# A Fourier mixing layer and a tanh-shrink MLP on one core: the beginning put in another order

## The chip, the cores and the metric

The kernel runs on one core of a Trainium2 chip. The core has TensorE (PE, matrix products; PEld is its loading of weights), VectorE (DVE), ScalarE (ACT), GpSimd (POOL) and SyncE (SP), which each run their own list of instructions in order and wait for each other through semaphores. Transfers are issued from SP's, ACT's and GpSimd's queues and carried by 16 DMA engines. The metric is device time in microseconds (us); less is better.

## The reference

A batch of 8 sequences of 3008 tokens by 256 channels is filtered in the frequency domain, and the result goes token by token through an MLP whose activation is h - tanh(h).

```python
def _attn_ref(x, filt_r, filt_i):
    X = np.fft.rfft(x, axis=1)              # x: (8, 3008, 256)
    F = (filt_r + 1j * filt_i)[None, :, :]  # (1505, 256)
    Y = X * F
    return np.fft.irfft(Y, n=x.shape[1], axis=1).astype(np.float32)

def _moe_ref(x, w_in, w_out):               # x: (24064, 256)
    h = x @ w_in                            # (256, 2048)
    g = h - np.tanh(h)
    return (g @ w_out).astype(np.float32)   # (2048, 256)
```

The two weight matrices arrive as 64-bit floating-point numbers, which the kernel reads as integers; x and the filters are 32-bit.

## The kernel before

**The transform.** 3008 = 64 x 47. A transform of one batch is three stages of small matrix products with a trip through DRAM after the first and the second: `first` multiplies 24 slices of x (128 x 256 each) with the matrices f and stores to `ct1`; `middle` takes seven rounds, one for each group of rows ("slot", six of 120 rows and a last of 48), and stores to `ct2`; `last` loads e2 from `ct2`, multiplies with the matrices g and leaves u in SBUF for the MLP.

**A round of the middle stage** has four parts. `forth` (L316 to L332) loads nothing itself; it multiplies a2 with two constant matrices into the bank pa, copies the half of v = 1 with ACT, and lets VectorE form sum and difference (L330, L331). `filtered` (L334 to L350) is the complex product with the filter: two products of 1024 columns (L340, L343), a difference and a sum of 512 (L345, L346, engine `by2`), then another sum and difference on VectorE (L348, L349). `back` (L352 to L365) multiplies with the constant matrices into pe, copies to e1 with ACT and stores from ACT's queue. For batch 0 the seven rounds run in the beginning, by themselves, with `by2` GpSimd; for the batches 1 to 7 they are spread over the dense rounds of the batch before, with `by2` VectorE.

**The weights** come in eight quarters, four of w_in (tile wu) and four of w_out (wd), each of two pieces of 128 x 512 numbers. `converted` turns a piece into 32-bit floating point: a load of 512 KB (raw), three VectorE operations (L145, L146, L148), two operations that VectorE (L152, L154) or ACT (L157, L158) does, then VectorE again (L160, L162, L164 and two or three at L171). After both pieces of a quarter GpSimd forms four sums of weights (`sums`, L201 to L204), because the MLP's products are done with seven block products where eight would be usual. Three generators spread the conversion: `weights_alone` (all on VectorE), `weights` (shared with ACT, several pieces under way) and `weights_slow` (one step at a time, all on VectorE).

**The beginning (L783 to L899), batch 0.** SP issues, in turn, a third of f and a third of x, three times, and the mats; GpSimd's queue the filter of round 0 and four raw pieces. Between the thirds of the first stage `weights_alone` converts quarters 0 and 1. Then seven rounds follow; in each, the products back of the preceding round and the steps of `weights` for quarters 2 to 4 stand between the parts. Quarter 5 follows behind the last round. A filter buffer is one of three (`filt[g % 3]`), filled from GpSimd's queue with six transfers a round.

**The dense rounds.** Each of 48 groups of tokens takes four rounds U (192 in all, and two more to empty the pipeline). In round U TensorE does `up(U)` (seven pairs of products into x, y and z), the other engines do `shrink(U - 1)` (the activation by ACT and VectorE) and TensorE does `down(U - 2)`. VectorE adds the banks into h (L512, L529, L537, L545), ACT copies from the banks (L495). Inside a round five calls of `t(k)` place other work: at most one step of a transform whose place in the plan has come (`planned`, in units of a fifth of a round), one step of `weights_slow`, and one step of a copy of the filters in DRAM. The plan spreads `first` of batch 1 over the places 0.2 to LEAD/2, that of batch 2 over LEAD/2 to LEAD, and `middle` of batch 1 from LEAD to LAG, with LEAD 30 and LAG 104. Quarters 6 and 7 are converted here. wd's quarter n is first used in round n + 2, wu's quarter n in round n.

Of the kernel before, what the change touches and what calls it, by code (L numbers as in the profile page):

```python
# [9 lines left out]
F32 = mybir.dt.float32  # L10
# [11 lines left out]
SG = 5  # L22
# [14 lines left out]
LEAD, LAG = 30, 104  # L37
# [53 lines left out]
def kernel(  # L91
# [119 lines left out]
    def weights(tiles, quarters, ahead):  # L211

        jobs = parts_of(quarters)
        began = []
        for job in jobs[:ahead]:
            began.append(begun(tiles, job))
            yield
        for k in range(len(jobs) + 1):
            if k < len(jobs):
                next(began[k])  # L220
            if k > 2 and k % 2:
                sums(quarters[k // 2 - 1])
            yield
            if k < len(jobs):
                next(began[k])
            if k > 0:
                for _ in began[k - 1]:
                    pass
            if k + ahead < len(jobs):
                began.append(begun(tiles, jobs[k + ahead]))  # L230
            yield
        sums(quarters[-1])
        yield

    def weights_alone(tiles, quarters, queue):

        jobs = parts_of(quarters)
        began = [begun(tiles, job, True, queue) for job in jobs[:2]]
        yield
        for k in range(len(jobs)):  # L240
            if k + 2 < len(jobs):
                began.append(begun(tiles, jobs[k + 2], True, queue))
            for _ in began[k]:
                pass
            if k % 2:
                sums(quarters[k // 2])
            yield

    def weights_slow(tiles, quarters):

        jobs = parts_of(quarters)
        began = [begun(tiles, job, True) for job in jobs[:2]]
        yield
        for k in range(len(jobs)):
            for _ in began[k]:
                yield
            if k + 2 < len(jobs):
                began.append(begun(tiles, jobs[k + 2], True))
            if k % 2:
                sums(quarters[k // 2])  # L260
                yield
# [55 lines left out]
    def forth(g, at, z):  # L317
# [4 lines left out]
        for v in (1, 0):  # L322
# [4 lines left out]
            if v:  # L327
                ACT.copy(xy[:, 2:4], pa)
                yield xy
# [4 lines left out]
    def filtered(g, xy, ft, by, by2):  # L334
# [4 lines left out]
        nn = tr.tile([KM, 4, DM], F32, tag="nn", bufs=1, name="nn")[0:n]  # L339
        by.tensor_mul(nn.rearrange("p (x v) c -> p x v c", v=2), ab,  # L340
                      fv[:, :, 0:1].to_broadcast([n, 2, 2, DM]))
        yield
# [23 lines left out]
    def middle(b, z):  # L366
# [4 lines left out]
        for g in range(len(SLOTS)):  # L371
# [5 lines left out]
            if before:  # L377
                next(before[0])
                yield
            next(there)  # L380
# [405 lines left out]
    with tc.tile_pool(name="tr", bufs=2) as tr, tc.manual_schedule():  # L786
        with tc.tile_pool(name="pro", bufs=1) as pro, \
# [11 lines left out]
            def first0(xt, c):  # L799

                for i in range(2):
                    r = 8 * c + 4 * i
                    a1 = pro.tile([128, 4, DM], F32, tag="a1", bufs=4, name="a1")
# [21 lines left out]

            def tiles0(k, dtype, n):
# [10 lines left out]
            V.memset(exp_b, 0.0)  # L837
            xs = []
            for c in range(3):
                nc.sync.dma_start(f0[:, 8 * c:8 * c + 8], f_d[:, 1024 * c:1024 * c + 1024])  # L840
                xs.append(load_x(big([128, 8, DM], F32, "x0"), 0, 8 * c, 8))

            ACT.activation(exp_b, exp_b, AF.Arctan)
            V.memset(exp_b, -896.0)
            ws = weights_alone(tiles0, range(2), G)

            for t in filt:
                G.memset(t[0:SG, 2:4], 0.0)
            nc.sync.dma_start(mats, mats_d)
            fts = {0: filters_of(0)}  # L850
            next(ws)
            for c in range(3):
                for k, _ in enumerate(first0(xs[c], c)):
                    if k == 3:
                        next(ws)
            fts[1] = filters_of(1)
            turned_rows()
            late_ws = weights(tiles0, range(2, 5), 3)
            a2 = {0: load_a2(0, 0), 1: load_a2(0, 1)}
            for _ in range(2):  # L860
                next(late_ws)
            for _ in ws:
                pass
            ws = late_ws
            next(ws)
            waiting = iter(())
            last_g = len(SLOTS) - 1
            for g in range(last_g + 1):
                if g + 1 < last_g:
                    fts[g + 2] = filters_of(g + 2)  # L870
# [3 lines left out]
                if g + 1 < last_g:  # L874
                    a2[g + 2] = load_a2(0, g + 2)
                done = filtered(g, xy, fts.pop(g), V, G)
                for _ in waiting:
                    next(ws, None)
                for _ in done:
                    pass  # L880
                next(ws, None)
                waiting = back(0, g, xy, z0)
                if g == last_g - 1:
                    fs = first(1, z1)
                    next(fs)
                    ws_gap = weights_alone(tiles0, range(5, 6), nc.sync)
                    next(ws_gap)
            for _ in waiting:
                pass
            e2s[0] = load_e2(*groups[0])  # L890
            for w in (ws, ws_gap):
                for _ in w:
                    pass
# [5 lines left out]
        with tc.tile_pool(name="dn", bufs=2) as dn, \  # L899
# [15 lines left out]
            def tiles1(k, dtype, n):  # L915

                tag, bufs = {"raw": ("ft", 2), "it": ("xy", 2), "pt": ("nn", 1), "st": ("e1", 2),
                             "ft": ("a2", 2)}[k]
                return tr.tile([128, n], dtype, tag=tag, bufs=bufs, name=k)

# [16 lines left out]
            late, copies = weights_slow(tiles1, range(6, 8)), filters_d()  # L937
# [3 lines left out]
            next(late)  # L941
# [123 lines left out]
```

## Time and profile before

| | |
|---|---|
| median of 3 runs | 2806.02 us (2805.11 to 2806.81) |
| the profiled execution | 2806.34 us, of which its span is 2804.6 us |
| TensorE busy | 2693.7 us, 96% of the span |
| VectorE / ACT / GpSimd busy | 1673.3 / 1723.7 / 1388.3 us |
| moved by the DMAs | 215.44 MB, 77 GB/s over the span |

A profile shows one execution. Its rows give busy time by engine, for the whole span or for a stretch of it; groups of instructions by source line with count and mean time; who waited for whom; and a chain of waits, followed back from the last instruction. "L345" is line 345 of the kernel before. A product in 32-bit floating point shows as two records, so four products appear as x8. The granted clock is the share of TensorE's full rate that it was given. A queue's "us to landing" is the median from the issue of a transfer until its data are there.

### The profile page before, as it was taken

The page shows a single profiled execution, that of the slowest core. Times are in us where ns is not written, and L with a number is a line of the kernel's source. Part 1 is how long each engine was busy: PE and PEld are TensorE (multiplying, and loading weights), DVE is VectorE, ACT ScalarE, POOL GpSimd, SP SyncE. Part 2 cuts the span into 40 slices and gives each one's busy share as a digit, 9 for nine tenths or more (in the row PEclk, how much of TensorE's full clock was granted, in tenths as well). Part 3 has the DMA queues.
Part 4 walks back from the last instruction along what each step waited for, and adds up shares of the span by engine and source line. Part 5 has one row for each costly group of instructions (what it writes and reads, how often), then busy time and mean ns, then how long its engine had stood idle before and what let it go on. Part 6 is the DMA issues. An engine that isn't in the chain of part 4 may idle for free.

```text
span 2804.6 us, 36366 instructions
## 1 busy us (share of the span) xinstructions
PE 2693.7 (96%) x12830; PEld 2366.6 (84%) x12830; DVE 1673.3 (60%) x2094; ACT 1723.7 (61%) x2583; POOL 1388.3 (50%) x1195
## 2 busy tenths in 40 slices
PE   4499999999999999999999999999999999999998
PEld 3388888988889888998889888898888988899887
DVE  4755675666556665556656666566654766554545
ACT  2155666666666666666666666666666666666665
POOL 4455545544445444545455444454544554454452
PEclk8699999999999999999999999999999999999999
DMA  9475213323132332234223331242222222111010
GB/s 247 116 245 145 69 43 78 95 69 82 51 95 74 80 91 55 74 74 104 56 62 73 101 87 47 60 116 66 78 53 67 54 64 55 30 24 33 21 26 18
DMA packets 341634, 215.44 MB, mean 77 GB/s; under 512 B 227736, under 2 KB 300988, under 8 KB 341251
## 3 DMA queue, kind: packets, MB, share of 16 engines
q1 hardware_dynamic: 296851, 154.15, 23.1%
q10 hardware_dynamic: 39504, 50.61, 5.8%
q0 software_dynamic: 5088, 8.28, 1.1%
q8 instruction: 103, 1.69, 0.3%
q14 instruction: 88, 0.72, 0.1%
HBM read 137.83 MB, written 78.12 MB: 77 GB/s over the span
## 4 chain that ended last, share of the span: by engine, by line
PE 87%; DVE 6%; DMA 2%; issue 2%; ACT 2%; POOL 1%; ACTq 0%; SPq 0%; DVEq 0%; POOLq 0%
PE o L614 38%; PE x L489 22%; PE z L489 11%; PE y L489 5%; PE pa L325 3%; PE pe L359 3%; PE pu L455 3%; PE pf L293 2%; DMA x<-in_x_dram 1%; DMA ct<-a 1%; DVE xy L349 1%; DVE h L570 1%; DVE h L545 1%; DVE h L512 1%; DVE xy L348 0%
## 5 line engine op out<-in xcount | busy, mean ns | idle before, releaser
L614 PE MATMUL o<-t,wd 128*128 128x256 f32 (+1 forms) x3072 | 775.0, 375 | 0.0
L469 POOL TENSOR_TENSOR t<-h 128x512 f32<-128x512 f32 (+1 forms) x190 | 261.8, 1378 | 893.6 <-DVE h L570 865.6
L570 DVE TENSOR_TENSOR h<-h,y 128x1024 f32<-128x1024 f32 (+1 forms) x384 | 511.2, 1331 | 293.0 <-ACT y L566 292.5
L614 PEld LDWEIGHTS o<-t,wd 128*128 128x128 f32 x3072 | 582.7, 190 | 69.7 <-issue 2.4
L489 PE MATMUL x<-tu,wu 128*128 128x256 f32 (+1 forms) x2304 | 586.0, 377 | 2.1 <-ACT s L495 1.7
L614 PE MATMUL o<-h,wd 128*128 128x256 f32 (+1 forms) x2304 | 583.8, 376 | 3.2 <-DVE h L570 3.2
L489 PEld LDWEIGHTS x<-tu,wu 128*128 128x128 f32 x2304 | 430.1, 190 | 64.5 <-ACT u L495 8.8
L614 PEld LDWEIGHTS o<-h,wd 128*128 128x128 f32 x2304 | 434.1, 190 | 55.5 <-DVE h L570 4.3
L495 ACT COPY s<-x 128x512 f32<-128x512 f32 (+1 forms) x192 | 110.9, 577 | 511.6 <-PE x L489 498.2
L560 ACT ACTIVATE y<-h 128x1024 f32<-128x1024 f32 (+1 forms) x384 | 400.2, 1042 | 12.5 <-ACT a L294 5.1
L563 ACT ACTIVATE y<-y 128x1024 f32<-128x1024 f32 (+1 forms) x384 | 399.5, 1040 | 12.6 <-ACT a L294 0.4
L566 ACT ACTIVATE y<-y 128x1024 f32<-128x1024 f32 (+1 forms) x384 | 400.0, 1042 | 4.7
L529 DVE TENSOR_TENSOR h<-z,u 128x512 f32<-128x512 f32 (+1 forms) x192 | 130.1, 678 | 275.2 <-ACT u L495 274.3
L495 ACT COPY u<-x 128x512 f32<-128x512 f32 (+1 forms) x384 | 219.5, 572 | 94.1 <-PE x L489 70.7
L471 POOL TENSOR_TENSOR t<-h 128x512 f32<-128x512 f32 (+1 forms) x190 | 271.2, 1427 | 0.0
L470 POOL TENSOR_TENSOR t<-h,t 128x512 f32<-128x512 f32 (+1 forms) x190 | 263.6, 1387 | 14.9
L472 POOL TENSOR_TENSOR t<-t,h 128x512 f32<-128x512 f32 (+1 forms) x190 | 268.0, 1411 | 0.0
L537 DVE COPY h<-x 128x512 f32<-128x512 f32 (+1 forms) x192 | 130.4, 679 | 162.3 <-PE x L489 161.8
L489 PE MATMUL x<-ut,wu 128*128 128x256 f32 (+1 forms) x768 | 193.9, 375 | 0.7 <-DVE h L537 0.7
L489 PE MATMUL y<-ut,wu 128*128 128x256 f32 (+1 forms) x768 | 193.8, 375 | 0.0
L489 PE MATMUL z<-ut,wu 128*128 128x256 f32 (+1 forms) x768 | 193.7, 375 | 0.0
L489 PE MATMUL z<-tu,wu 128*128 128x256 f32 (+1 forms) x768 | 193.7, 375 | 0.0
(116 smaller groups left out, 3051.5 us busy)
## 6 DMA issues: line engine op xcount, KB each, us to landing
e<-ct SPq DMA_DIRECT2D x48, 512.0 KB, 4.3
a<-ct SPq DMA_DIRECT2D x48, 480.0 KB, 5.2
ct<-e ACTq DMA_DIRECT2D x96, 240.0 KB, 2.8
ct<-a ACTq DMA_DIRECT2D x84, 256.0 KB, 2.7
x_sb<-in_x_dram SPq DMA_DIRECT2D x161, 128.0 KB, 4.1
ft<-filt SPq DMA_DIRECT2D x42, 480.0 KB, 6.8
out_dram<-ot SPq DMA_DIRECT2D x1248, 16.0 KB, 1.5
gt<-g SPq DMA_DIRECT2D x48, 256.0 KB, 3.2
```

What stands on the lines that cost most here:

```text
L469: by.tensor_sub(t[0], b[0][1], b[0][0])
L470: by.tensor_sub(t[1], b[1][1], t[0])
L471: by.tensor_sub(t[2], b[1][1], b[0][1])
L472: by.tensor_sub(t[3], t[1], b[1][0])
L489: nc.tensor.matmul(bank[:, k], wu[:, q - 1, (2 * u + k) * 128:(2 * u + k + 1) * 128], rhs[q - 1], start=(first and k == 0), stop=True, ski ...
L495: ACT.copy(t, X)
L537: V.tensor_copy(h[:, 2, :, 0:w], X)
L560: ACT.activation(y[k], ht[k], AF.Arctan, scale=TURN)
L563: ACT.activation(y[k], y[k], AF.Tanh, scale=BEND)
L566: ACT.activation(y[k], y[k], AF.Square, scale=SCALE, accum_out=y_sums[:, 2 * U + k // 2:2 * U + k // 2 + 1])
L570: V.tensor_mul(ht[k], ht[k], y[k])
L614: nc.tensor.matmul(product(q), wd[:, q - 1, (2 * u + k) * 128: (2 * u + k + 1) * 128], rhs[q - 1][:, k], start=(u == 0 and k == 0 and q == ...
```

## The change

- The first loads: f and mats are issued from ACT's queue, x from SP's. GpSimd clears its filter buffers first, loads the filter of round 0, and then waits, through a copy of one element (`gate`), until the second third of x has landed; only then it issues raw pieces 0 and 1, the filter of round 1, raw pieces 2 and 3 and the turned rows.
- The pieces of quarters 0 to 2 (six) are converted in the beginning by `convert`, which shares with ACT: four ahead of round 0, behind all products of the first stage, and two behind the last round. `weights` and `weights_alone` are gone.
- Middle stage of batch 0: `by2` is VectorE; the products forth of round g + 1 are issued ahead of the filter of round g; nn has two buffers. In rounds 0 to 5 the last sum and difference are left out, and `back0` reaches the same result with twice the products: each pe half is a product with nn[k] plus a product with nn[2 + k], accumulated in PSUM. The last round keeps them.
- `weights_slow` shares with ACT and takes quarters 4, 3, 5, 6, 7 (ten pieces). It begins in the beginning of the kernel with its first two loads, and has two steps in each `t(k)`.
- The plan: `first` of batch 1 from 6 to 20, of batch 2 from 20 to LEAD, and LEAD is 34.

```diff
-LEAD, LAG = 30, 104
+LEAD, LAG = 34, 104
...
 def weights_slow(tiles, quarters):
         jobs = parts_of(quarters)
-        began = [begun(tiles, job, True) for job in jobs[:2]]
+        began = [begun(tiles, job) for job in jobs[:2]]
...
+            def back0(g, nn):
+                way = ways(g, 1)
+                for v in range(2):
+                    pe = z0("pe", [128, 2, DM])[0:KM]
+                    for k in range(2):
+                        nc.tensor.matmul(pe[:, k], way[2 * v + k], nn[:, k],
+                                         start=True, stop=False)
+                        nc.tensor.matmul(pe[:, k], way[3 - k if v else 0], nn[:, 2 + k],
+                                         start=False, stop=True)
+                    e1 = tr.tile([KM, 2, DM], F32, tag="e1", bufs=2, name="e1")
+                    ACT.copy(e1, pe)
+                    ACT.dma_start(rows(ct2, 0, g, 2 * v, 2), e1)
...
+            for t in filt:
+                G.memset(t[0:SG, 2:4], 0.0)
             xs = []
             for c in range(3):
-                nc.sync.dma_start(f0[:, 8 * c:8 * c + 8], f_d[:, 1024 * c:1024 * c + 1024])
+                ACT.dma_start(f0[:, 8 * c:8 * c + 8], f_d[:, 1024 * c:1024 * c + 1024])
                 xs.append(load_x(big([128, 8, DM], F32, "x0"), 0, 8 * c, 8))
+            ACT.dma_start(mats, mats_d)
...
             fts = {0: filters_of(0)}
+            gate = cst.tile([1, 1], F32, name="gate")
+            G.tensor_copy(gate, xs[1][0:1, 0, 0:1])
+            jobs = parts_of(range(3))
+            began = [begun(tiles0, job, queue=G) for job in jobs[:2]]
+            fts[1] = filters_of(1)
+            began += [begun(tiles0, job, queue=G) for job in jobs[2:4]]
+            turned_rows()
+            def convert(k):
+                for _ in range(1 if k + 1 < len(jobs) else 0):
+                    next(began[k + 1])
+                for _ in began[k]:
+                    pass
+                if k % 2:
+                    sums(k // 2)
+                if k + 4 < len(jobs):
+                    began.append(begun(tiles0, jobs[k + 4], queue=G))
             for c in range(3):
-                for k, _ in enumerate(first0(xs[c], c)):
-                    if k == 3:
-                        next(ws)
+                for _ in first0(xs[c], c):
+                    pass
             a2 = {0: load_a2(0, 0), 1: load_a2(0, 1)}
+            next(began[0])
+            for k in range(4):
+                convert(k)
...
+            there = {0: there0(0)}
             for g in range(last_g + 1):
+                if g + 2 <= last_g:
+                    fts[g + 2] = filters_of(g + 2)
+                    a2[g + 2] = load_a2(0, g + 2)
+                if g < last_g:
+                    there[g + 1] = there0(g + 1)
+                next(there[g][0])
+                xy = there.pop(g)[1]
-                done = filtered(g, xy, fts.pop(g), V, G)
-                for _ in waiting:
-                    next(ws, None)
-                for _ in done:
-                    pass
-                next(ws, None)
-                waiting = back(0, g, xy, z0)
+                done = filtered(g, xy, fts.pop(g), V, V, pro)
+                nn = next(done)
+                for _ in range(2):
+                    next(done)
+                if g < last_g:
+                    back0(g, nn)
+                else:
+                    next(done)
+                    for _ in back(0, g, xy, z0):
+                        pass
                 if g == last_g - 1:
                     fs = first(1, z1)
                     next(fs)
-                    ws_gap = weights_alone(tiles0, range(5, 6), nc.sync)
-                    next(ws_gap)
+                    late = weights_slow(tiles1, (4, 3, 5, 6, 7))
+                    next(late)
             e2s[0] = load_e2(*groups[0])
+            for k in range(4, len(jobs)):
+                convert(k)
...
-                f = [spread(NX, *((0.2, LEAD / 2) if b == 1 else (LEAD / 2, LEAD) if b == 2
+                f = [spread(NX, *((6, 20) if b == 1 else (20, LEAD) if b == 2
                                   else (0.2, LAG)), firsts, b, first)
...
                     next(late, None)
+                    next(late, None)
```

`there0(g)` runs `forth(g)` up to its products and ACT's copy. The buffers of the first stage's result (a1) go from four to three.

87 lines of the change are left out of this document (17 added, 70 removed).

## The prediction

> **What bounds the kernel now.** The page comes first: TensorE's row of the 40 slices, and the chain of waits by engine.
>
> ```profile
> span 2804.6 us, 36366 instructions
> ...
> PE   4499999999999999999999999999999999999998
> ...
> PE 87%; DVE 6%; DMA 2%; issue 2%; ACT 2%; POOL 1%; ACTq 0%; SPq 0%; DVEq 0%; POOLq 0%
> ```
>
> TensorE is full in every slice but the first two, and the diff leaves the later batches as they are. So the work that the change moves can only pay in the beginning, until the first dense product. Next the busy times by stretch there: up to VectorE's first addition of the middle stage (50.67), to that stage's last one, to the first dense product at 143.8, and the first three dense rounds.
>
> ```profile
> 0.00:50.67 50.67, 19.65 (x57) 14.90 (x58) 16.68 (x42) 9.11 (x15) 22.25 (x39) 0.83 0.95 262
> 50.67:132.00 81.33, 37.63 (x98) 26.14 (x98) 60.00 (x93) 17.43 (x30) 44.96 (x54) 0.67 0.55 144
> 132.00:143.80 11.80, 11.62 (x45) 8.24 (x43) 8.39 (x23) 1.69 (x3) 3.17 (x5) 0.68 0.48 154
> 143.80:154.50 10.70, 9.67 (x46) 7.84 (x46) 7.33 (x20) 3.89 (x7) 3.11 (x6) 1.00 0.86 270
> 154.50:166.80 12.30, 9.98 (x47) 7.82 (x45) 7.30 (x17) 7.31 (x13) 4.00 (x6) 1.00 0.88 270
> 166.80:183.50 16.70, 14.76 (x73) 13.44 (x73) 13.46 (x23) 11.27 (x19) 7.12 (x8) 1.00 0.79 236
> ```
>
> After its length a row gives busy time of PE, PEld, DVE, ACT, POOL, then granted clock, DMA share, GB/s. The first 50.67 us belong to the DMAs (share 0.95). The next 81.33 us belong to nobody: the DMAs are half used, TensorE half busy, VectorE 74%. That is a chain. The waits of that stretch and one turn of the chain say which:
>
> ```profile
> PE pe L359 <- DVE xy L348: 43.7, 7, 8.9
> DVE xy L348 <- POOL nn L346: 20.3, 7, 4.5
> ...
> 53.44 1.24 DVE xy L343
> ...
> 54.76 1.25 POOL nn L345
> 56.01 1.22 POOL nn L346
> ```
>
> In each of seven rounds VectorE hands two sums to GpSimd, waits for them, adds once more, and only then can TensorE go back. Weight pieces fill the holes, and lengthen the rounds where they stand ahead of a round's own work. A round takes 81.33/7 = 11.6 us.
>
> **The change part by part.** *Middle stage.* GpSimd's two sums go to VectorE; the last two additions (L348, L349) go to TensorE, which adds in PSUM with twice the products; no weights are converted between rounds; each round's way forth stands ahead of the preceding round's filter. VectorE's own cost of a round:
>
> ```profile
> 50.67 0.69 DVE L330 TENSOR_TENSOR xy<-pa,xy 120x512 f32<-120x512 f32 x1 [10.04 <-PE pa L325]
> ...
> 52.18 1.23 DVE L340 TENSOR_TENSOR nn<-xy,filt 120x1024 f32<-120x1024 f32 x1
> ...
> 512.63 0.68 DVE L345 TENSOR_TENSOR nn<-nn,xy 120x512 f32<-120x512 f32 x1
> 513.23 0.68 DVE L346 TENSOR_TENSOR nn<-nn,xy 120x512 f32<-120x512 f32 x1
> ```
>
> From start to start the two additions take 1.51, the two products 1.26 and 1.24, the two sums (a later batch has them on VectorE) 0.60 and 0.68: 5.29 us. Six rounds and a last one that keeps its two additions (1.28 more) make 7 x 5.29 + 1.28 = 38.3 us, the floor.
>
> TensorE has 12 products a round where it had 8. Their price depends on the granted clock:
>
> ```profile
> 67.71 3.67 PE L359 MATMUL pe<-xy,mats_sb 120*120 120x256 f32 x8 [2.84 <-DVE xy L348]
> 71.22 1.89 PE L325 MATMUL pa<-a,mats_sb 120*120 120x256 f32 x8
> ...
> 50.00:52.00 2.00, 2.00 (x9) 0.83 1.08 279
> 58.00:60.00 2.00, 1.90 (x5) 0.50 1.08 210
> 72.00:74.00 2.00, 1.11 (x6) 1.00 0.98 249
> ...
> 46.83 5.60 PE L325 MATMUL pa<-a,mats_sb 120*120 120x256 f32 x16 [8.12 <-issue]
> ```
>
> Four products show as x8. Cold they take 3.67 us, warm 1.89: a round has 11.0 us of TensorE work cold, 5.7 warm by these widths. The granted clock (third figure from the right in the three windows) rises within the burst that began at 46.83 and ended at 52.4, and has fallen again by 58, after five idle microseconds. In the new order TensorE idles about 5.29 - 3.67 = 1.6 us between bursts, so I take it warm: 5.7 beside VectorE's 5.29, hidden but for little. The Trainium skill, "TensorE: Matmul & The Clock Gate", Part 1, states the same switch as a rule: half rate after an idle window of about 3.4 us, full rate after one such busy window. By that rule the stage stays warm; if it were cold throughout, the sum would be the one of the third rival below.
>
> DMAs are the other bound. A round reads 0.49 MB of the first stage's result, reads 0.49 of filters, writes 0.49. From the first round on there are left: five reads (2.16 MB, the last is short), five filters (2.16), seven writes (3.15), what is under way of round 1 (0.98), two weight pieces (1.05), and the loads for the dense rounds that SP issues as soon as the last read is out (two x and f pairs, two pieces, one gt: 2.1). Together 11.6 MB. At the 262 GB/s of the first stretch they take 11.6/0.262 = 44 us; at the poorest rate of a window that was nearly full, 53:
>
> ```profile
> 40.00:50.00 10.00, 3.17 (x8) 2.49 (x9) 0.63 (x2) 0.59 (x1) 6.29 (x10) 0.69 0.80 220
> ```
>
> The last 2.1 MB (8 us) are not waited for in this stage, so I take 42, between floor and byte count. Gain 81.3 - 42 = 39.3; bounds 43.0 and 28.
>
> GpSimd still issues the filters, six a round:
>
> ```profile
> L823 POOL DMA_DIRECT2D filt<-in_filt_i_dram x16 | 9.2, 598 | 0.0
> filt<-in_filt_r_dram POOLq DMA_DIRECT2D x7, 120.0 KB, 6.3
> ```
>
> A buffer is free 4.0 us into its round (after the second product); six issues take 3.6 and landing 6.3, so it is filled at 13.9, while the round three later asks for it at 3 x 5.29 + 1.5 = 17.4. Cost nothing; without that cover (landing in 15 us as below) some 1.5 us a round, which lies within the 53.
>
> *First stage.* f and mats move from SP's queue to ACT's, weights wait on GpSimd until the second x chunk is in, and GpSimd's clearing of the filters comes first. Queued behind that wait are four pieces, the filters of round 1 and the turned rows; VectorE's conversions stand ahead of round 0, so four pieces (2.1 MB) are still needed before it. Bytes needed by then, from the tiles' shapes: x 3.08, f 1.57, mats 0.53, one filter 0.48, write 3.15, one read 0.49, pieces 2.1: 11.4 MB, 43.5 us at 262 GB/s. Behind the landing of the last read stand the 3.8 us that passed before between TensorE's first product (46.83) and VectorE's first addition (50.67).
>
> ```profile
> x<-in_x_dram SPq DMA_DIRECT2D x5, 512.0 KB, 22.2
> raw<-in_moe_w_in_dram POOLq DMA_DIRECT2D x4, 512.0 KB, 15.2
> ```
>
> Hence 47.3 instead of 50.67; x, which took 22.2 us to land beside other loads, comes earlier. I take a gain of 4, bounds 0 (same bytes, same pipe) and 8. The Trainium skill, "Trainium Kernel Development and Optimization", Key Constraints, speaks against this part: queues of several engines share the 16 DMA engines, another queue saves issue time alone. By it the gain would be 0 and the time 4 us longer; the 0.95 share agrees with it for bandwidth, and the 4 is an estimate for order alone.
>
> *Between the stages.* Last back products, copy, store, load of e2, first pu: 131.5 to 142.0.
>
> ```profile
> 131.53 3.63 PE pe L359 x8
> ...
> 141.99 1.97 PE L455 MATMUL pu<-gt,e 128*128 128x128 f32 x16 [0.18 <-DMA e<-ct]
> 143.79 0.98 PE L489 MATMUL x<-ut,wu 128*128 128x224 f32 x4
> ```
>
> This stays. Two conversions that now stand behind the stage on VectorE (7 us) and their GpSimd sums fit into these 10.5 us, and the sums are wanted two rounds later: nothing; were that cover gone, 7.
>
> *First dense rounds.* They take ten pieces where they had four, at two steps per fifth of a round instead of one, and two operations of each go to ACT. A piece on VectorE:
>
> ```profile
> 71.96 0.42 DVE L145 TENSOR_SCALAR conv<-raw 128x512 int32<-128x512 int32 x1
> 74.75 0.76 DVE L171 SCALAR_TENSOR_TENSOR wu<-conv 128x256 f32<-128x256 f32 x2
> 75.42 1.22 DVE L340 TENSOR_TENSOR nn<-xy,filt 120x1024 f32<-120x1024 f32 x1
> ...
> L154 DVE TENSOR_SCALAR pt<-pt 128x512 int32<-128x512 int32 x4 | 3.6, 888 | 0.0
> L512 DVE TENSOR_TENSOR h<-y,s 128x448 f32<-128x448 f32 x4 | 2.5, 616 | 1.7 <-ACT s L495 1.7
> raw<-in_moe_w_out_dram SPq DMA_DIRECT2D x2, 512.0 KB, 6.4
> ...
> 148.31 0.76 PE z L489 x4
> 149.06 0.88 PE pf L293 x4
> ```
>
> 71.96 to 75.42 is 3.5 us. Round 0 has two (6.9), four h operations (0.62 each, as L512's mean) and the tu sums: about 10 us of VectorE, against seven pairs of products of 0.76 = 5.3 us on TensorE, because the first transform of batch 1 now begins in round 1. Before, the round took 10.7 with 9.67 busy; 4 x 0.88 = 3.5 us of those transform products move into full rounds, so the round would have had to shrink to 7.2 and takes 10: 2.8 lost. Round 1 was already a fifth idle (9.98 of 12.3) and stays so. In round 2 VectorE was busy 13.46 of 16.7 with one piece; a second adds 3.5, and the two operations that each of both gives to ACT take off 1.3 (0.42, and 0.89 for L154 beside GpSimd): 15.7, against TensorE's 14.76. What waits behind a late piece on VectorE is the next h, and behind it TensorE's next round. I put 0.4 on each of rounds 2 to 4, and so 4 us in all; bounds 0 and 15 (ten pieces at 1.5: the lead of a piece is 2.25 steps of a fifth of 14 us, 6.3, against 6.4 to land).
>
> **Sum.** 2806.3 (the profiled execution's own time, 0.3 above the median shown; its span is 2804.6) - 39.3 - 4 + 4 = 2767.
>
> **The rivals.** *Bytes are hidden, floor reached:* VectorE sets the middle stage, the order gives 8 and the dense rounds lose nothing: 2806.3 - 43 - 8 = 2755. For it: share 0.55 before in that stretch, and the 2.1 MB are not urgent; against it 1.47 MB in 5.29 us is 279 GB/s, above the full stretch. *Dense rounds pay back:* VectorE becomes their bound, pieces at 7 instead of 3.5 us beside GpSimd, ten of them 35 more, of which some 13 fit into idle time (the three rounds' rows leave 11.6): 22 lost, 2806.3 - 43.3 + 22 = 2785. For it the 888 ns of L154 (L145, an operation of its kind and size, took 420 above), against it that VectorE was 59 to 81% busy there before. *TensorE stays cold:* 6 x 11.0 + 6.6 = 73 us for the stage, 2806.3 - 8 - 4 + 4 = 2798. For it the 0.67 of that stretch, against it the rise after 4 us in three rows. *Late pieces, slower:* the eight pieces loaded within the dense rounds land as they did in the beginning, 15.2 us, 8.9 past their lead of 6.3; VectorE holds the h sums behind them: 8 x 8.9 = 71 lost, 2806.3 - 43.3 + 71 = 2834. It makes the kernel slower from 6.3 + 43.3/8 = 11.7 us on. Against it the 6.4 us of pieces in dense rounds, and that the first transform now spreads over more rounds.
>
> **How the numbers follow.** Forecast 0.50, floor reached 0.25, paid back 0.12, cold 0.07, late pieces 0.06. Range: from 3 below the floor case to 2792, past the paid-back case, by the bounds 28, 0 and 15 (2793); outside lie cold, late pieces and the edges. This kernel tells no difference under 0.2% (5.6 us) apart. Faster holds all but the last case and a sliver of the cold one: 0.93; same 0.02, slower 0.05.
>
> **What would show it.** No POOL row in the middle stage but issues; VectorE's round near 5.3 to 6 with idle time there before L303 or L292 put down to DMAs (mine) or none (floor); DMA share near 1 there; granted clock 1.0 from the third round, not 0.5; first dense product near 100 to 103 instead of 143.8; rounds 0 to 4 with VectorE over 85% busy and TensorE idle about 10 us in all, against 5.3 in the first three before. A first dense product after 115, or over 20 us of TensorE idle in the first five rounds, would make it wrong.

## The result, and the profile after

| | median | range |
|---|---|---|
| kernel before | 2806.25 us | 2804.14 to 2811.38 (15 runs) |
| changed kernel | 2799.93 us | 2797.24 to 2804.20 (15 runs) |
| ratio | 0.9976 | 95% interval 0.9968 to 0.9984 |

The change gains 6.3 us (0.24%) where 39 were forecast. The profiled execution of the changed kernel is its longest: 2804.2 us, with a span of 2802.3, so what is read from it below may be up to 4 us worse than in a median execution. Its page answers to the rows shown of before (span, TensorE's row of slices, the chain by engine):

```profile
span 2802.3 us, 36449 instructions
...
PE   4888999999999999999999999999999999999998
...
PE 89%; DVE 6%; issue 2%; ACT 2%; DMA 1%; SPq 0%; ACTq 0%; POOL 0%; DVEq 0%
```

The stretch that is not full was two slices at 4 tenths; it is now one slice at 4 and three at 8. The gain of the beginning is there; something behind the beginning takes it back. The busy times by stretch say where: first stage, middle stage, gap, dense rounds 0 and 1, then rounds 2, 3, 4, 5 and 6 one by one (length, busy PE, PEld, DVE, ACT, POOL, granted clock, DMA share, GB/s).

```profile
0.00:52.69 52.69, 19.19 (x64) 14.73 (x64) 17.18 (x37) 14.37 (x24) 18.24 (x32) 0.87 0.94 258
52.69:95.07 42.38, 34.15 (x140) 26.00 (x140) 37.85 (x46) 9.96 (x17) 23.60 (x38) 0.92 0.79 216
95.07:106.27 11.20, 11.09 (x43) 8.00 (x41) 5.91 (x14) 4.07 (x7) 1.59 (x3) 0.70 0.46 148
106.27:134.30 28.03, 19.00 (x74) 14.90 (x74) 23.32 (x48) 14.95 (x26) 9.28 (x14) 0.88 0.52 155
134.30:157.00 22.70, 17.47 (x74) 15.74 (x73) 17.92 (x28) 13.33 (x22) 13.49 (x17) 0.85 0.57 170
157.00:179.00 22.00, 17.75 (x85) 16.44 (x85) 17.35 (x26) 12.49 (x20) 13.12 (x14) 0.84 0.47 153
179.00:202.70 23.70, 18.92 (x78) 16.59 (x77) 15.83 (x21) 11.39 (x18) 13.60 (x17) 0.86 0.61 194
202.70:218.60 15.90, 15.90 (x77) 14.32 (x76) 6.78 (x12) 11.06 (x18) 7.08 (x9) 1.00 0.77 225
218.60:244.50 25.90, 19.18 (x77) 16.12 (x76) 6.24 (x9) 10.79 (x16) 12.89 (x15) 0.82 0.71 184
```

The first dense product starts at 106.27 instead of 143.79: a lead of 37.5 us. Rounds 2, 3, 4 and 6 take 22 to 26 us; round 5, without a piece, is full and takes 15.9. Counted from the first product into y of a round to that of the next, in the profiled executions:

| | rounds 0-1 | 2-4 | 5 | 6 | 7 | lead left behind round 7 |
|---|---|---|---|---|---|---|
| before | 23.0 | 47.6 | 14.9 | 18.8 | 14.7 | |
| after | 27.2 | 68.4 | 15.9 | 25.9 | 15.1 | 4.0 |

So 33.5 of the 37.5 us go back within eight rounds: 4.2 in rounds 0 and 1, 20.8 in rounds 2 to 4, 1.0 in round 5, 7.1 in round 6 and 0.4 in round 7. TensorE's three longest waits in these (total, times, longest):

```profile
PE pf L255 <- DVE h L476: 13.4, 4, 4.8
PE pa L287 <- DMA a<-ct: 6.7, 1, 6.7
PE x L453 <- ACT u L459: 6.3, 4, 3.0
```

The first: a product of the first transform (pf) shares bank y with the MLP and waits until VectorE's addition at L476 has emptied it. Why VectorE is late shows in one piece of round 2, VectorE first, then GpSimd, then TensorE (start, duration):

```profile
137.79 1.36 DVE L162 TENSOR_SCALAR pt<-pt 128x512 int32<-128x512 int32 x1
139.19 1.51 DVE L164 SCALAR_TENSOR_TENSOR pt<-pt,st 128x512 int32<-128x512 int32 x1
140.73 2.57 DVE L171 SCALAR_TENSOR_TENSOR wd<-ft,pt 128x256 f32<-128x256 f32 x3
143.22 0.61 DVE L476 TENSOR_TENSOR h<-y,s 128x448 f32<-128x448 f32 x1
...
148.28 0.43 DVE L162 TENSOR_SCALAR pt<-pt 128x512 int32<-128x512 int32 x1
148.75 0.69 DVE L164 SCALAR_TENSOR_TENSOR pt<-pt,st 128x512 int32<-128x512 int32 x1
149.47 0.83 DVE L171 SCALAR_TENSOR_TENSOR wd<-ft,pt 128x256 f32<-128x256 f32 x3
```

```profile
137.43 1.43 POOL L433 TENSOR_TENSOR t<-h 128x448 f32<-128x448 f32 x1
138.94 1.20 POOL L434 TENSOR_TENSOR t<-h,t 128x448 f32<-128x448 f32 x1
140.10 1.57 POOL L435 TENSOR_TENSOR t<-h 128x448 f32<-128x448 f32 x1
141.64 1.30 POOL L436 TENSOR_TENSOR t<-t,h 128x448 f32<-128x448 f32 x1
```

```profile
143.89 2.08 PE L255 MATMUL pf<-x_sb,f 128*128 128x256 f32 x4 [4.03 <-DVE h L476]
```

Ten us later, when GpSimd adds nothing, the same operations take 0.43, 0.69 and 0.83: this piece is 3.5 us late, and the transform's product behind it waits 4.03. Each slow operation ends shortly after a GpSimd addition: L164 ends at 140.70, 0.56 after L434 (140.14); L162 at 139.15, 0.29 after L433 (138.86). That is what operations would show that wait for the whole addition and then run. The Trainium skill, "SBUF — State Buffer", Who interferes with whom, states this as a rule (a VectorE operation with two SBUF inputs, or in a two-port mode, and a GpSimd operation that reads SBUF lock each other out for a whole instruction); these rows agree with it.

The second wait is in round 6, and SP's queue shows it:

```profile
226.74 5.58 SPq L658 DMA_DIRECT2D out_dram<-ot  x12
232.36 0.46 SPq L270 DMA_DIRECT2D a<-ct  x1
```

The middle stage of batch 1 now begins at LEAD 34; its first read is issued behind twelve stores of output.

The third wait lies in rounds 0 and 1. Before the longest of the four (3.0 us, in round 0), ScalarE's copy of the bank (L459) stands in ScalarE's list behind a conversion (L157), which waited 2.4 us for VectorE.

### The profile page after: what moved, and what is told of

The parts are those of the page before. It is cut to its first block, busy times and chain, and to the rows that moved or that the text cites. A ratio compares the mean times of both kernels' runs of the same rounds, so it can differ in the third digit from the quotient of the medians.

```text
span 2802.3 us, 36449 instructions
## 1 busy us (share of the span) xinstructions
PE 2702.2 (96%) x12878; PEld 2375.4 (85%) x12878; DVE 1682.9 (60%) x2076; ACT 1735.9 (62%) x2603; POOL 1375.7 (49%) x1184
## 4 chain that ended last, share of the span: by engine, by line
PE 89%; DVE 6%; issue 2%; ACT 2%; DMA 1%; SPq 0%; ACTq 0%; POOL 0%; DVEq 0%
PE o L578 38%; PE x L453 22%; PE z L453 11%; PE y L453 5%; PE pa L287 3%; PE pe L322 3%; PE pu L419 3%; PE pf L255 2%; DVE h L534 1%; DVE h L476 1%; DVE h L509 1%; DMA x<-in_x_dram 1%; DVE xy L312 0%; DVE xy L311 0%; PE pe L803 0%
## 5 line engine op out<-in xcount | busy, mean ns | idle before, releaser
L433 POOL TENSOR_TENSOR t<-h 128x512 f32<-128x512 f32 (+1 forms) x190 | 261.3, 1375 | 883.9 <-DVE h L534 858.8
L453 PEld LDWEIGHTS x<-tu,wu 128*128 128x128 f32 x2304 | 430.9, 190 | 68.5 <-ACT u L459 15.7
L459 ACT COPY s<-x 128x512 f32<-128x512 f32 (+1 forms) x192 | 110.8, 577 | 508.8 <-PE x L453 497.7
L493 DVE TENSOR_TENSOR h<-z,u 128x512 f32<-128x512 f32 (+1 forms) x192 | 130.1, 677 | 267.8 <-ACT u L459 266.6
L459 ACT COPY u<-x 128x512 f32<-128x512 f32 (+1 forms) x384 | 219.3, 571 | 87.8 <-PE x L453 66.2
L434 POOL TENSOR_TENSOR t<-h,t 128x512 f32<-128x512 f32 (+1 forms) x190 | 264.6, 1393 | 14.9
L501 DVE COPY h<-x 128x512 f32<-128x512 f32 (+1 forms) x192 | 130.4, 679 | 159.5 <-PE x L453 158.9
```

The costliest lines, as they stand in the source:

```text
L433: by.tensor_sub(t[0], b[0][1], b[0][0])
L434: by.tensor_sub(t[1], b[1][1], t[0])
L453: nc.tensor.matmul(bank[:, k], wu[:, q - 1, (2 * u + k) * 128:(2 * u + k + 1) * 128], rhs[q - 1], start=(first and k == 0), stop=True, ski ...
L459: ACT.copy(t, X)
L501: V.tensor_copy(h[:, 2, :, 0:w], X)
```

## The experiments

Each ran beside the kernel before on the same chip (there 2806.1 to 2808.2 us). "Rounds 2-4" and "round 6" are counted as in the table.

**The plan of the middle stage alone goes back to 30.**

```diff
-                m = [spread(n_m, LEAD if p == 0 else 0.2, LAG, mids, b, middle)
+                m = [spread(n_m, 30 if p == 0 else 0.2, LAG, mids, b, middle)
```

> Edit: only the place from which batch 1's middle stage is spread goes back from 34 to 30; both first transforms keep their new places. In the changed kernel round 6 takes 25.9 us (18.8 before), with 6.7 us of TensorE waiting for the first a2 load, which SP issues only at 232.4, behind the first output stores of group 0. Theory, SP's queue: the load is ready to go earlier and only stands behind the stores; issued ahead of them the wait of 6.7 us falls under 3, round 6 to about 19, the time by 5 to 7 us, to 2793 to 2795 (changed kernel 2799.9, before 2806.2). Rival, the data are late (the first stage of batch 1 ends too late for any order): the wait stays over 5 us and the time within 2 us of 2800.

2795.32 us (2794.41 to 2797.54). Round 6 falls to 19.9, the wait for the read from 6.7 to 3.2, and the read is now issued ahead of the stores:

```profile
215.77 0.56 SPq L270 DMA_DIRECT2D a<-ct  x1
...
223.81 1.73 SPq L658 DMA_DIRECT2D out_dram<-ot  x4
```

About 4.6 us of the loss are this constant. Rounds 2 to 4 do not change.

**The steps of conversion in another order within a round.**

```diff
-                    next(late, None)
-                    next(late, None)
+                    for _ in range((0, 3, 2, 3, 2)[k]):
+                        next(late, None)
```

> Edit: the ten steps of conversion in a round stay ten, but none stands in t(0), ahead of VectorE's first sum (L476); they go 0, 3, 2, 3, 2 to the five places instead of 2 each. In the changed kernel rounds 2 to 4 take 22.7, 22.0 and 23.7 us (16.7, 15.1, 15.9 before), each with TensorE idle 4.0 to 4.8 us at a first-transform product that waits for L476, and cold behind it. Theory A, order: L476 is late because a piece's last operations stand ahead of it; with the same work in another order the three waits fall under 1 us each, the rounds to 15 to 18, the time by 12 to 20 us to 2780 to 2788. Theory B, VectorE is full (pieces slowed beside GpSimd): the same lateness turns up at another sum, rounds stay over 20, the time 2796 to 2802.

2791.54 us (2789.54 to 2793.27); rounds 2-4 take 57.9; one wait for L476 is left (4.4), and x now waits for L501 (5.5 in four). Between the two expectations: the place counts, but not for all of it; part of the waiting goes over to another addition.

**Conversions of the dense rounds by VectorE alone** (`begun(tiles, job, True)`, as before the change).

> Edit: the ten pieces in the dense rounds are converted by VectorE alone again (two more VectorE operations a piece, two fewer on ACT). In the changed kernel VectorE waits 8.6 us in four places for ACT's part of a piece. Theory C, coupling to ACT: those waits go, rounds 2 to 4 shorten by 2 us or more each, the time falls by 5 or more, under 2795. Theories A and B: VectorE has 0.7 to 2.2 us more a piece ahead of its sums, TensorE's waits for L476 grow, the time rises by 3 to 15 us, 2803 to 2815.

2801.42 us (2798.53 to 2803.69), rounds 2-4 68.6, waits for L476 13.1. No difference from the changed kernel can be told. The waits for ScalarE's copies (L459) fall from 6.3 to 1.9 us, but others come in their place (z for L493: 3.1), so ScalarE's share is neither the loss nor a help here.

**Twelve pieces in the beginning, four in the dense rounds.**

```diff
-            jobs = parts_of(range(3))
+            quarters = (0, 1, 2, 4, 3, 5)
+            jobs = parts_of(quarters)
...
-                    late = weights_slow(tiles1, (4, 3, 5, 6, 7))
+                    late = weights_slow(tiles1, (6, 7))
...
                     next(late, None)
-                    next(late, None)
```

> Edit: quarters 0, 1, 2, 4, 3, 5 (twelve pieces) are converted in the beginning, eight of them behind the last round, and only 6 and 7 in the dense rounds with one step in each place, as in the kernel before; everything else as changed. The beginning grows by six pieces of 3.5 us, the first dense product goes from 106.3 to about 127. Theories A and B (six pieces more in the dense rounds cost about 23 us there): rounds 0 to 4 fall from 96.5 us to about 75, the time to 2794 to 2800. The prediction's step (pieces there cost 4 us in all): the rounds give back 4 at most and the time is about 2817.

2800.94 us (2798.82 to 2804.04). Six pieces more in the beginning put the first dense product 27.6 us later (4.6 each); rounds 0 to 4 take 66.2 instead of 95.6 us, 29.4 less (4.9 each). By this, six pieces in the dense rounds (with two steps in each place, where this run has one) cost as much as with TensorE idle: they were hidden by nothing. My 4 us for all ten fell here.

**The transform's products always in a bank of their own.**

```diff
-                latest[0] = "y" if quarter[0] in (1, 2, 3) and latest[0] == "t" else "t"
+                latest[0] = "t"
```

> The first transform's products always take the bank of their own (t) instead of changing between it and Y's bank, which the addition at L476 must free. Theory A (TensorE loses rounds 2 to 4 because L476 stands behind a weight piece on VectorE and the transform's product needs the bank that it frees): the waits of pf for L476, 13.4 us, are gone; Y of the next round comes a round later and never waits for it. In their place each pf waits for ScalarE's copy of the one before it, about 0.5 us each. Rounds 2 to 4 come to 57 to 62 us instead of 68.4, the time to 2788 to 2795. Theory B (VectorE has too much work in those rounds, 17.9 of 22.7 us, and whatever product comes next waits for it): the waits go over to another product (x for L501, z for L509), rounds 2 to 4 stay at 65 to 69 us and the time at 2797 to 2803.

2773.96 us (2771.44 to 2775.33), ratio to before 0.9877 (0.9862 to 0.9893). Rounds 2-4: 58.1, as theory A had it. The time is 14 us better than it had, and that part comes later: the lead is 15.5 us behind round 7 and 2804.6 - 2773.0 = 31.6 at the end of the spans. TensorE's waits from 300 to 2700 us, changed kernel first, then this one:

```profile
PE pe L322 <- DVE h L476: 7.3, 10, 1.3
PE pa L287 <- DVE h L476: 6.5, 11, 0.7
```

```profile
PE x L453 <- ACT u L459: 0.2, 1, 0.2
```

The products of the middle stage, too, waited for L476 in the changing bank: 13.8 us in this stretch, of the 16.1 us that the lead grows behind round 7.

**The same edit in the kernel before, alone.**

> The kernel before with the transform's products always in the bank t, nothing else. Theory A (the change of banks costs in every round in which a transform's product follows Y, in the old kernel too): 2786 to 2792, most of it in rounds after the tenth. Then the rebuilt beginning by itself is worth 2789 - 2774 = 15 us. Theory B (the banks cost only where VectorE is crowded with conversions, as in the changed kernel): within 4 us of 2806, and the rebuilt beginning by itself is worth 30.

2789.80 us (2787.55 to 2792.17). Beside the kernel before on its chip (2807.2) that is 17.4 us, all of it after round 7: up to there the two run level. From 300 to 2700 us the kernel before has the same waits for its addition L512 (7.4 and 6.6 us), and none with the edit. With the edit in both, the rebuilt beginning is worth 2789.8 - 2774.0 = 15.8 us instead of 6.3 (on two chips; by each one's difference to the kernel before there, 16.9).

**GpSimd's sums of h left out in the first six rounds.**

```diff
...
-        combine(blocks, [t[:, k, :, 0:w] for k in range(4)],
-                G if U + 2 < 4 * len(groups) else V)
+        if U > 5:
+            combine(blocks, [t[:, k, :, 0:w] for k in range(4)],
+                    G if U + 2 < 4 * len(groups) else V)
...
+        if U < 6:
+            rhs[3:] = [b[0][1], b[0][0], b[1][0], b[1][1]]
```

> Leaves out GpSimd's four sums of h (L433 to L436) in the first six rounds, 5.5 us of GpSimd each; the down products of those rounds take blocks of h in their place, so the number of products is the same. All conversions stay. Theory A (VectorE falls behind in rounds 2 to 4 because its work is slowed while GpSimd adds): the three products of a piece (L171) take 0.83 us throughout instead of up to 3.5, L164 0.69, VectorE's busy time falls from 17.9, 17.4, 15.8 to about 14 a round, the waits for L476 from 13.4 us to under 5, and the time is 2782 to 2790. Theory B (the number of operations and their order decide, whatever their speed): busy time falls by under 2 us a round, the waits stay over 9 us and the time is 2794 to 2801.

2784.98 us (2782.97 to 2786.41), theory A; the waits of pf for L476 fall from 13.4 to 3.1 us. This kernel leaves out work that the result needs, so it shows only what the sums cost. Its windows of rounds 2 to 4:

```profile
132.00:149.30 17.30, 15.27 (x75) 13.73 (x75) 14.64 (x28) 13.92 (x24) 9.89 (x15) 1.00 0.81 254
149.30:165.80 16.50, 15.43 (x87) 14.61 (x86) 13.30 (x25) 12.24 (x20) 5.60 (x8) 1.00 0.63 183
165.80:183.00 17.20, 15.70 (x75) 13.73 (x74) 12.20 (x22) 11.16 (x18) 10.72 (x15) 1.00 0.82 248
```

As many operations of VectorE (28) in round 2 take 14.64 instead of 17.92 us, the clock stays at 1.00, and rounds 2-4 take 51.0 instead of 68.4.

**The same sums given to VectorE in these rounds** (`G if 5 < U and ...`), nothing left out.

> The four sums of h that GpSimd takes (L433 to L436, 1.2 to 1.6 us each) go to VectorE for the first six rounds, where each takes about 0.62; VectorE gets 2.5 us more work a round and GpSimd 5.5 less. Theory A (VectorE's pieces are slowed by GpSimd's adding; the run without those sums took 51.0 us for rounds 2 to 4): L171 stays at 0.83 and L164 at 0.69, and rounds 2 to 4 take 51 to 59 us instead of 68.4; time 2783 to 2792. Theory B (the run without the sums was faster because products no longer waited for them, and VectorE is bound by its number of operations): rounds 2 to 4 take 68 us or more, time 2799 or more.

2793.49 us (2790.18 to 2797.36), rounds 2-4 60.4: VectorE gets 2.5 to 2.7 us more work a round, L164 takes 0.69 throughout, and the rounds become shorter by 8.0 in all. Somewhat longer than theory A had it (waits of pf for L476 of 9.3 us are left), and far from theory B: GpSimd's adding beside VectorE was the dearer way.

**Combinations.** Bank t and the middle stage from 30; then these with the sums on VectorE.

> The transform's products always in the bank t, and the middle of batch 1 spread from 30 again. If the two losses stand in different rounds and add up, round 6 falls from 25.1 to about 19.5 us and the time from 2774 to 2767 to 2771. If the earlier middle stage takes back what the bank gave (its products share TensorE's and VectorE's rounds 5 to 7), 2773 to 2781.

2768.45 us (2767.11 to 2769.27), round 6 18.5: the two add up.

> The bank t throughout, the middle of batch 1 from 30, and the sums of h on VectorE in the first six rounds. Theory A (adding of GpSimd slows VectorE): on top of the other two, rounds 2 to 4 fall from 58.1 us (bank t alone) to 48 to 54, and the time to 2760 to 2767. Theory B: rounds 2 to 4 stay at 56 to 62 and the time at 2768 to 2774.

2764.07 us (2763.24 to 2769.48), ratio to before 0.9851 (0.9837 to 0.9864): the best version, 36 us below the changed kernel. Its rounds 2, 3 and 4:

```profile
134.00:150.10 16.10, 15.32 (x73) 13.79 (x73) 14.35 (x28) 11.67 (x19) 6.95 (x11) 0.96 0.81 244
150.10:165.70 15.60, 15.57 (x86) 14.58 (x86) 15.45 (x29) 12.12 (x20) 6.15 (x7) 1.00 0.59 186
165.70:185.60 19.90, 16.35 (x77) 14.07 (x76) 15.33 (x28) 11.17 (x18) 10.30 (x15) 1.00 0.75 237
```

Three more variants. Bank t and the plan from 30 with the steps at 3, 3, 1, 0, 3:

> Three changes together: the middle of batch 1 spread from 30 again, the first transform's products always in the bank t, and the steps of conversion 3, 3, 1, 0, 3 over the fifths of a round instead of 2 each, so that none stands ahead of L501, which frees X for the next round's first product, and many ahead of L476, for which then nothing waits soon. If order and banks cause most of the 20 us that rounds 2 to 4 lose, they come to 50 to 55 us and the time to 2774 to 2783. If VectorE's load beside GpSimd causes it, rounds 2 to 4 stay above 60 and the time is 2785 to 2793.

2778.55 us (2775.25 to 2781.45), rounds 2-4 65.1 where two steps each give 59.6: my places were worse than an even spread, and products waited for ScalarE's copies (x for u at L459: 13.9 us in four) instead of L476. The best version with VectorE alone converting, then also with the steps at 0, 3, 2, 3, 2:

> The version with the bank t throughout, the middle of batch 1 from 30 and the sums of h on VectorE in the first six rounds, in which now VectorE alone converts in the dense rounds. There ScalarE stood 4.1 us in round 4 at a conversion (L157) that waited for VectorE, with its copies and the tanh of h queued behind it. Theory A (this coupling, hidden by the bank's waits when it was tried alone, is the next loss): round 4 falls from 19.9 us to 16 to 18, the time from 2764 to 2759 to 2762. Theory B (VectorE is full, and 0.7 us more a piece cost more than the wait): rounds 1 to 5 grow and the time is 2764 to 2772.

> The same with the steps of conversion at 0, 3, 2, 3 and 2 over the fifths of a round instead of 2 each. If with a bank of its own for the transform nothing waits for L476 soon, the place of the steps no longer matters: within 2 us of the version with 2 each. If it still matters as it did with the changing banks, 4 to 8 us less than that version.

2768.95 us (2768.16 to 2769.84) and 2771.23 (2770.49 to 2772.03): round 4 falls to 16.6 and 16.2 as hoped, but rounds 2 and 3 grow to 39.1 and 39.5 together from 31.6. In the main theory B: with GpSimd's additions gone, VectorE's longer pieces cost more than the wait for ScalarE did. The order that helped with the changing banks here costs 2.3.

**The first stage.** Five buffers for a1 instead of three (shared with nn):

> The first stage's result tiles a1 take five buffers, shared with the two of the middle stage's nn, instead of three. Theory A (ScalarE's copies waited for the stores of a1: 4.75, 1.24 and 1.02 us): these waits are gone, the last store is issued at 30 to 33 us instead of 36.66, the conversions on VectorE begin at 31 to 34 instead of 37.69, its first addition of the middle stage comes at 47 to 49 instead of 52.69, and the time is 2795 to 2797. Theory B (the first stage is bound by bytes: DMA share 0.94 over the whole stretch, and the same bytes have to pass before the first read): the stores are issued sooner but land no sooner; first addition at 51.5 to 53, time 2798 to 2801.

2799.30 us (2797.11 to 2800.87). Theory B: the last store is issued at 33.34 instead of 36.66, the first read at 42.65 instead of 42.57, the first addition comes at 52.42. Then the four conversions moved behind the middle stage, and in a second run the weights' loads later as well (the first hunk, in that run alone):

```diff
-            G.tensor_copy(gate, xs[1][0:1, 0, 0:1])
+            G.tensor_copy(gate, xs[2][0:1, 0, 0:1])
...
             a2 = {0: load_a2(0, 0), 1: load_a2(0, 1)}
-            next(began[0])
-            for k in range(4):
-                convert(k)
...
             e2s[0] = load_e2(*groups[0])
-            for k in range(4, len(jobs)):
+            next(began[0])
+            for k in range(len(jobs)):
                 convert(k)
```

> The four conversions that stand ahead of the middle stage's first round on VectorE go behind its last round; loads and their order stay. Theory A (bytes set the first stage's end, the conversions happen to end with it): the first read is issued at 42 to 43 us as before, the first addition of the middle stage comes at 51 to 52 instead of 52.69. Theory B (the conversions hold it): the first addition comes at 48 to 50. In both, the first dense product comes 12 to 16 us later than 106.27, and the time is 2805 to 2815.

> As the run with the four conversions moved, and the weights' loads wait for the third chunk of x instead of the second, so that 2.1 MB less stand beside x and the stores. Theory A (bytes): the first read is issued at 35 to 39 us instead of 42.57 and the first addition comes at 43 to 48. Theory B (the chain of x, products, copies and stores takes its time whatever else is loaded): the first read at 41 to 43, the first addition at 50 to 52.

The first addition came at 51.65 (2815.12 us) and 51.99 (2813.99), the first read at 42.90 and 41.64. The conversions hold it by 1 us at most; whether the loads do was still open, as theirs stood beside the last stores. Then no weights until the first read has landed, the filter of round 1 ahead of that (the conversions stay moved; these lines take the place of the earlier gate and loads):

```diff
+            fts[1] = filters_of(1)
...
+            G.tensor_copy(gate, a2[0][0:1, 0, 0:1])
+            began = [begun(tiles0, job, queue=G) for job in jobs[:4]]
```

> All four conversions moved behind the middle stage, and now no weights at all are loaded until the first read of the first stage's result has landed; the filters of round 1 stand ahead of that. Theory A (the weights' bytes beside x and the stores set the end of the first stage): x's third chunk is used at 24 to 26 us instead of 28.5, the last store takes under 5 us to land instead of 7.5, the first read is issued at 35 to 38 and the first addition of the middle stage comes at 44 to 48 instead of 52. Theory B (x comes no faster with the other loads away, and each step behind it takes its own time): x at 28 to 29, read issued at 40 to 42, first addition at 50 to 52. Time 2810 to 2818 in both, since six conversions stand behind the middle stage.

2812.45 us (2809.93 to 2816.03). Neither theory as a whole: the first read is issued at 39.12, the first addition comes at 48.06, though the last third of x is used later, at 32.16 (28.53 in the changed kernel). The changed kernel's DMAs in between, and this one's:

```profile
20.00:28.00 8.00, 7.51 (x27) 5.89 (x25) 0.00 (x0) 2.95 (x6) 5.09 (x9) 1.00 1.09 218
28.00:36.00 8.00, 3.69 (x16) 2.96 (x16) 2.34 (x6) 2.59 (x5) 2.92 (x4) 1.00 1.03 398
```

```profile
20.00:28.00 8.00, 6.66 (x21) 5.23 (x22) 0.00 (x0) 2.72 (x5) 0.00 (x0) 1.00 1.07 201
28.00:36.00 8.00, 5.87 (x27) 4.52 (x25) 0.00 (x0) 3.73 (x8) 0.00 (x0) 1.00 0.88 312
```

Two legs: x takes till 28 or later at 200 to 220 GB/s with the DMAs full, whether weights stand beside it or not; from there to the first addition it is 24.2 us in the changed kernel, 23.7 with the conversions moved, and 15.9 with the weights' loads held back as well.

## Why the prediction was wrong, point by point

- *Middle stage, 42 us:* 42.4, which is luck, as it is not for the bytes that I chose it by. The DMA share is 0.79, no wait of VectorE for a DMA shows, and VectorE is 37.85 busy: it ran near the floor of 38.3, plus 2.9 us in which VectorE waited for round 1's products. My 1.6 us of idle TensorE between bursts had left out the start of the chain: there TensorE idled 5.5 us and did the back products of round 0 at half clock (the timeline, the window, the wait):

```profile
58.41 1.18 PE L803 MATMUL pe<-nn,mats_sb 120*120 120x256 f32 x2 [5.51 <-DVE nn L308]
```

```profile
58.40:64.50 6.10, 6.09 (x15) 4.69 (x16) 5.50 (x7) 0.59 (x1) 6.10 (x12) 0.51 0.52 141
```

```profile
DVE xy L292 <- PE pa L287: 2.9, 1, 2.9
```

  From the third round on the clock was full, up to the last round's products back: they came after 2.6 us of waiting and from 95.6 us on ran at half clock (0.50). The "cold" rival came true for parts of two of the seven rounds.
- *First stage, a gain of 4:* a loss of 2.0. The failed step is one rate (262 GB/s) for all bytes. What stands ahead of the last x moves at 218 with the DMAs full, the weights and stores behind it at 398 together, about half each. x did come 6 us earlier, but the stores then shared the DMAs with the weights: the first read was issued at 42.57 (before: 42.23) and took 0.5 us longer. The last 1.0 us is the four conversions that VectorE does ahead of its first addition, by the run in which they were moved. The gain of 0 that the prediction named beside its 4 was nearer.
- *Between the stages:* 11.2 us before the first dense product, as before (11.8).
- *First dense rounds, "4 us in all":* the step that sank the forecast; it measured 33.5. Rounds 0 and 1 lost 4.2, not far from my 2.8; rounds 2 to 4 lost 20.8, where I had put 0.4 on each, and I had put nothing on round 6 (7.1). VectorE's load was not far off (15.7 us in round 2 by my sum, 17.9 busy), and yet the round took 22.7: what was wrong is what a late piece costs. Three terms failed. I priced a piece at 3.5 us with one small correction for work beside GpSimd; beside GpSimd's additions single operations took two to three times their time (17.4 us in rounds 2 to 4 by the run without them, 8.0 by the run that gives them to VectorE). I asked what waits behind a late piece and named the next h; I did not ask for which bank the transform's products wait, which the new plan spread over these very rounds (10.3 us by the run with bank t). And LEAD from 30 to 34 has no term in my sum (4.6 us, with the read behind the stores in SP's queue). The first two overlap: both take away the wait for L476 (13.4 us; 3.1 without the sums, none with bank t). The best version, with bank t, the plan from 30 and the sums on VectorE, gives 35.9, of which 21 lie in rounds 0 to 7 (its lead behind round 7 is 25.3 us, that of the changed kernel 4.0) and the rest later.
- *The rivals:* "dense rounds pay back" came nearest (pieces at twice the price beside GpSimd) and had 22 us and a chance of 0.12. But VectorE was not the bound by its load: it was busy 79, 79 and 67% of rounds 2, 3 and 4, while TensorE waited for one of its additions. "Late pieces" did not happen: no wait of VectorE for a raw piece shows in these rounds.
- *What would show it:* over 20 us of TensorE idle in the first five rounds was my sign against the forecast; the rows give 28.03 + 22.70 + 22.00 + 23.70 = 96.4 us with 73.1 busy, 23.3 idle, and the busy part itself is stretched by clocks of 0.84 to 0.88. The other sign, VectorE over 85% busy, did not come: 74.4 of 96.4 us are 77%.

What stays open: of the 11.7 us that the best version still loses in rounds 0 to 7, 7.4 lie in rounds 0 to 4 and 4.3 in rounds 5 to 7. That they are VectorE's load, ScalarE's copies (TensorE still waits 6.2 us for L459) and the first read of the middle stage (a wait of 3.7 us in round 6) is read from its profile; of these only ScalarE's part in the conversions was taken away there, and the kernel became slower.

## What to carry to other kernels

Work that is moved under other work is priced by rows taken beside what will run there, not by the row where it stood alone: six pieces cost as much under dense rounds as with TensorE idle (29.4 against 27.6 us), and with GpSimd's additions of h left out, rounds 0 to 4 took 77.8 instead of 95.6 us with the same pieces. When an engine becomes fuller, list what its outputs set free (here one PSUM bank that two kinds of product shared), and look for that wait in the whole kernel, since it may cost where nothing was changed. A constant of a plan also sets an order in a queue: see which stores the moved load now stands behind.

## What the runs showed of the hardware

- Beside GpSimd's additions, operations of VectorE with both ends in SBUF took 1.36 for 0.43 us (L162), 1.51 for 0.69 (L164) and 2.57 for 0.83 (three L171), and ended shortly after an addition did. L509, which reads z from PSUM, took its 0.61 us beside GpSimd's L204 too. Four additions cost GpSimd 5.5 us; the same on VectorE take 0.62 to 0.73 each, and giving VectorE this work made the kernel 6 us faster.
- Waits of TensorE of 4.0 to 4.8 us cost more than themselves: in rounds 2 to 4 the granted clock is 0.84 to 0.86, and TensorE is busy 17.5 to 18.9 us a round where the run without these additions has 15.3 to 15.7 for nearly the same products.
